# Thresholded attention, then a squared-ReLU layer on one core: one chain of weight sums moved across the end of each pass, and sums of x moved by one or two products

## The chip, the cores and the metric

The kernel runs on one core of a Trainium2 chip. The metric is the device time of one execution in microseconds (us), lower is better. Before the change three runs took 1284.32 to 1285.13 us, with a median of 1284.76. The engines are PE (TensorE, matmuls and their weight loads), DVE (VectorE), ACT (ScalarE), POOL (GpSimd) and SP (SyncE, which here only issues DMAs). Each engine executes its own instructions in the order in which the program lists them; semaphores make one wait for another.

## The reference

```python
scores = scale * np.matmul(q, k.transpose(0, 1, 3, 2))        # 8 x 8 heads of 576 x 64
thresh = np.max(scores, axis=-1, keepdims=True) - tau
scores = np.where(scores >= thresh, scores, -1000000000.0)
attn = softmax(scores)                                        # with 1e-9 added to the sum
x = matmul(attn, v), heads joined to 4608 tokens x 512
h = np.maximum(x @ w_in, 0.0)                                 # 512 -> 2048
out = (h * h) @ w_out                                         # 2048 -> 512
```

Everything is float32.

## The kernel before, in words

The kernel has three stages: attention (to about 494 us of the profile), the first layer (x times w_in, 494 to 884 us), and the second layer (to the end). The change lies in the first layer.

Both layers multiply in Winograd's form of Strassen's scheme, in two levels: a 2 x 2 block product is made of 7 products instead of 8, at the price of sums of blocks ahead of it and behind it. With two levels there are 7 x 7 = 49 products, an outer index m and an inner index k. The loop over m goes in the order `OUTER = (1, 2, 6, 7, 4, 5, 3)`, and within one m the function `inner` (line 734) takes k in the order 1, 6, 7, 5, 2, 4, 3.

The 4608 tokens are taken in nine passes of 49 products; product 7i + j of a pass is the j-th of the i-th m. A product of passes 1 to 6 is 4 matmul instructions of 256 columns on the profile, one of passes 0, 7 and 8 is 8 of 128 columns. Passes 1 and 2 share one set of x (set 1), passes 3 and 4 set 2, passes 5 and 6 set 3; pass 7 has set 4.

Within one m the four PSUM banks X, Y, Z and W are used as follows. Product 0 fills X, and ACT copies it out (`p1`, line 769). Product 1 fills Y, and DVE adds p1 to it (`u2`). Product 2 fills Z, and DVE adds u2 (`u3`). Product 3 fills W, and DVE adds u3. Product 4 adds into X, product 5 into Z, product 6 into W, each followed by a DVE addition. So product 5 of an m, which writes into Z again, must wait until DVE has read Z for u3; product 6 must wait until DVE has read W. These DVE additions are line 128 with `ph` as input. Results that also need a kept sum get a POOL addition (line 128 on POOL, 128 x 512). m = 1 has none of these, m = 5 has six, the others three. The m of 2, 4, 5 and 3 give outputs: each output is put through ReLU and Square by ACT (lines 916 and 917) five products later and stored by SP (line 920).

Three kinds of extra work ride along, at product numbers written out by hand:

- *Chains of weight sums* (`chain_out`, line 1179). For the second layer's weights 44 chains run during the first layer: SP loads four 128 x 128 blocks at the chain's first product (line 1191), POOL makes four subtractions at its products 6, 7, 8 and 9 (line 1194, which shows as line 125, 128 x 128), and SP stores four blocks at its product 10 (line 1196). Two buffers alternate, so a chain's load waits until the store of the chain two before it has landed. `CHAINS` (line 1177) begins chains at products 0, 6, 12, 18, 24 and 30 of a pass (in pass 0 only the last three, in pass 7 the first five).
- *Sums of x* (`plan` and `summed`, lines 1200 to 1214). Set i + 1 is summed while set i is in use, from product 8 of a pass with an even number on, and on through the first products of the set's own first pass ("54" is product 5 of the next pass). Each sum has two steps: ACT copies one operand into PSUM (`c`, line 879) at the product written in the plan, and DVE subtracts (line 125 with `c`) two products later, or at the next sum's number if that comes sooner. There are two `c` buffers. In a plan's entry, `out_` is a sum of outer blocks, `in_` a sum of inner blocks of the m's named, and the last numbers name the sum.
- *Loads of x* (`load_set`, line 824, shown as line 837) on SP's queue. For sets 2 and 3 they stand at products 35 of the pass before, 7, 21 and 28.

Within one product's tick the order in the program is: chain instructions, DVE steps of sums that are due, new loads of x and new ACT copies, and then at most one ReLU and Square with its store.

Of the kernel before, what the change touches and what calls it, by code (L numbers as in the profile page):

```python
# [48 lines left out]
def kernel(  # L49
# [38 lines left out]
    NSTEP = B * S // STEP  # L88
# [75 lines left out]
    def made_at(m):  # L164
        return 4 + MADE.index(m) if m in MADE else RAW.index(m)
# [961 lines left out]
    with tc.manual_schedule():  # L1127
# [46 lines left out]
        chain_at = 26 * BANK  # L1174
        chains = [((0, RAW.index(k)), c) for k in RAW for c in range(4)]
        chains += [((1, made_at(m)), c) for c in range(4) for m in OUTER]
        CHAINS = [49 * n + 6 * c for n in range(NSTEP - 1) for c in range(3 if n == 0 else 0, 6)][0 : len(chains)]
        QUARTER = BANK // 4
        def chain_out(n, tick):

            for c, begins in enumerate(CHAINS):
                s_ = 49 * n + tick - begins
# [17 lines left out]
        def plan(i, at, loads, work):  # L1200
            for t, ms in loads.items():
                NEXT.setdefault(at + t, []).append(lambda ms=ms: load_set(i, ms))
            for t, (what, *args) in work.items():
                NEXT.setdefault(at + t, []).append(lambda what=what, args=args: summed(lambda: what(i, sum_v, *args)))
# [7 lines left out]
        def summed(copied):  # L1212
# [1 line left out]
            open_sum.append((clock["n"], copied()))  # L1214

        out_, in_ = sum_outer, sum_inner
        tail = {
            54: (out_, 4, 0), 56: (in_, (6, 7), 5), 58: (in_, (6, 7), 6), 60: (in_, (6, 7), 7), 62: (in_, (6, 7), 4), 65: (out_, 4, 1),
            68: (in_, (4, 5), 5), 70: (in_, (4, 5), 6), 72: (in_, (4, 5), 7), 74: (in_, (4, 5), 4),
            78: (in_, (3,), 5), 81: (in_, (3,), 6), 83: (in_, (3,), 7), 85: (in_, (3,), 4),  # L1220
        }
        plan(1, 0, {0: (7, 1, 3, 2)}, {
            10: (in_, (1,), 5), 12: (in_, (1,), 6), 14: (in_, (1,), 4), 16: (out_, 5, 0), 19: (out_, 5, 1), 21: (in_, (1,), 7),
            23: (out_, 6, 0), 26: (out_, 6, 1), 29: (out_, 7, 0), 31: (out_, 7, 1),
# [2 lines left out]
        for i in (2, 3):  # L1227
            plan(i, (2 * i - 2) * 49, {-14: (1,), 7: (7,), 21: (2,), 28: (3,)}, {
                8: (in_, (1,), 5), 10: (in_, (1,), 6), 12: (in_, (1,), 4), 15: (out_, 5, 0), 18: (out_, 5, 1), 21: (in_, (1,), 7),
                27: (in_, (2,), 5), 29: (in_, (2,), 6), 31: (in_, (2,), 7), 33: (in_, (2,), 4),  # L1230
                35: (out_, 6, 0), 37: (out_, 7, 0), 39: (out_, 6, 1), 41: (out_, 7, 1), **tail,
            })
        four = (1, 7, 2, 3)
        plan(4, 6 * 49, {-14: (1, 7), 7: (3, 2)}, {
# [124 lines left out]
```

## Time and profile before

| | |
|---|---|
| median of three runs | 1284.76 us |
| the profiled execution | 1284.26 us |
| span from its first to its last instruction | 1282.3 us |
| PE busy in the span | 1254.7 us, 98% |
| DVE, ACT, POOL busy | 999.9, 856.0, 895.6 us |
| first layer, from 493.99 to 884.23 us | 390.24 us, PE busy 388.23 |
| in it DVE, ACT, POOL busy | 305.60, 254.54, 325.86 us |

A row of the timeline gives the start, the length, the engine, the line, the operation with what it writes and reads, how many like it follow without a break (x3), and in brackets the idle time of the engine ahead of it with what ended that idle time. A row of the windows gives a stretch and its length, the busy time of an engine in it with the number of instructions, the granted TensorE clock, the mean busy share of the DMA engines and what they moved.

### The profile page before, as it was taken

The numbers are of one execution on the slowest core, as the hardware profiler recorded it, in microseconds if no ns is written. First come the engines' busy times: TensorE is split into PE (matmuls) and PEld (weight loads), VectorE is DVE, ScalarE is ACT, GpSimd is POOL, SyncE is SP. The second block draws the span as 40 slices with busy tenths as digits, with TensorE's granted clock in tenths as the row PEclk, the third lists the DMA queues.
The fourth block names the chain that finished last, engine by engine and source line by source line (L and its number), as shares of the span: only waits on it lengthen the run. The fifth ranks groups of instructions, "written<-read, shape, count | busy, mean of one in ns | idle before, by whom it ended". The sixth has DMA issues, their size and how long they took to land. (4 is left out here: it accounts for less than half of the span.)

```text
span 1282.3 us, 44206 instructions
## 1 busy us (share of the span) xinstructions
PE 1254.7 (98%) x17459; PEld 1086.2 (85%) x17459; DVE 999.9 (78%) x2449; ACT 856.0 (67%) x1552; POOL 895.6 (70%) x1094
## 2 busy tenths in 40 slices
PE   8998999999999999999999999999999999999998
PEld 6666666677777768988888788999999999999998
DVE  6999999999999997787878777877745664565463
ACT  6999999999999995666765766667423431343240
POOL 2565655655555557888797889758777867786775
PEclk9999999999999999999999999999999999999999
DMA  5565666544333413556666566589645314522411
GB/s 151 156 157 158 159 197 185 147 96 113 89 82 83 99 33 98 166 166 213 190 194 207 174 197 190 173 311 396 214 132 165 125 54 153 165 87 84 161 35 33
DMA packets 256591, 191.89 MB, mean 150 GB/s; under 512 B 96000, under 2 KB 217344, under 8 KB 256384
## 3 DMA queue, kind: packets, MB, share of 16 engines
q1 hardware_dynamic: 254928, 188.63, 49.3%
q8 instruction: 137, 2.24, 0.7%
q14 instruction: 70, 0.57, 0.1%
q10 hardware_dynamic: 1456, 0.44, 0.1%
HBM read 116.65 MB, written 72.35 MB: 147 GB/s over the span
## 5 line engine op out<-in xcount | busy, mean ns | idle before, releaser
L128 POOL TENSOR_TENSOR arena<-arena 128x512 f32<-128x512 f32 (+1 forms) x314 | 377.6, 1221 | 129.6 <-DVE arena L128 100.2
L1085 PE MATMUL po<-wall,arena 128*128 128x128 f32 x3528 | 394.4, 275 | 0.2 <-DVE arena L125 0.2
L1085 PEld LDWEIGHTS po<-wall,arena 128*128 128x128 f32 x3528 | 394.1, 192 | 0.4 <-DVE arena L125 0.4
L946 PE MATMUL ph<-arena,wall 128*128 128x128 f32 (+1 forms) x2352 | 388.2, 328 | 2.5 <-DVE arena L128 1.4
L946 PEld LDWEIGHTS ph<-arena,wall 128*128 128x128 f32 x2352 | 354.1, 191 | 36.6 <-DVE arena L128 4.5
L128 DVE TENSOR_TENSOR arena<-ph,arena 128x512 f32<-128x512 f32 x378 | 255.2, 689 | 76.4 <-PE ph L946 47.3
L125 POOL TENSOR_TENSOR arena<-arena 128x128 f32<-128x128 f32 (+2 forms) x314 | 254.8, 812 | 29.6 <-DMA arena<-w 11.2
L879 ACT COPY c<-arena 128x512 f32<-128x512 f32 (+2 forms) x319 | 176.1, 558 | 105.3 <-DVE arena L125 87.6
L128 DVE TENSOR_TENSOR arena<-po,arena 128x128 f32<-128x128 f32 x378 | 108.4, 290 | 168.3 <-PE po L1085 168.0
L473 ACT ACTIVATE arena<-arena 128x576 f32<-128x576 f32 x288 | 225.7, 871 | 17.4 <-DVE arena L463 17.4
L478 DVE SCALAR_TENSOR_TENSOR arena<-arena 128x576 f32<-128x576 f32 x288 | 225.8, 813 | 0.8 <-POOL arena L470 0.8
L463 DVE TENSOR_SCALAR_CACHE_REDUCE arena<-sc 128x576 f32<-128x576 f32 x288 | 204.4, 752 | 14.0 <-ACT arena L535 6.5
L125 DVE TENSOR_TENSOR arena<-arena,c 128x512 f32<-128x512 f32 (+2 forms) x283 | 177.0, 634 | 9.8 <-ACT c L879 8.7
L544 PEld LDWEIGHTS sc<-arena 64*64 64x64 f32 x5760 | 144.4, 133 | 44.7 <-DVE arena L463 42.1
L445 PE MATMUL sc<-arena 64*64 64x64 f32 (+1 forms) x2304 | 169.3, 415 | 1.8 <-DVE arena L665 1.7
L544 PE MATMUL sc<-arena 64*64 64x128 f32 (+1 forms) x5760 | 160.5, 262 | 10.3 <-DVE arena L463 7.8
L535 ACT COPY arena<-pt 128x1024 f32<-128x1024 f32 x144 | 159.2, 1105 | 1.6 <-PE pt L388 1.5
L769 ACT COPY arena<-po 128x128 f32<-128x128 f32 x63 | 16.6, 263 | 185.4 <-PE po L1085 185.4
L388 PEld LDWEIGHTS pt<-ident,arena 64*128 64x128 f32 x2304 | 83.0, 139 | 41.7 <-ACT arena L535 33.5
L445 PEld LDWEIGHTS sc<-arena 64*64 64x64 f32 x2304 | 62.1, 133 | 48.8 <-issue 22.8
L388 PE MATMUL pt<-ident,arena 64*128 64x64 f32 x2304 | 100.8, 227 | 2.4 <-ACT arena L535 2.0
L470 POOL TENSOR_SCALAR arena<-arena,tau_p 128x2 f32<-128x2 f32 x144 | 65.2, 453 | 41.9 <-DVE arena L463 35.1
(51 smaller groups left out, 919.4 us busy)
## 6 DMA issues: line engine op xcount, KB each, us to landing
g<-arena SPq DMA_DIRECT2D x144, 256.0 KB, 2.6
arena<-g SPq DMA_DIRECT2D x144, 256.0 KB, 5.0
w<-arena SPq DMA_DIRECT2D x60, 256.0 KB, 2.6
wall<-w SPq DMA_DIRECT2D x49, 256.0 KB, 5.3
arena<-w SPq DMA_DIRECT2D x44, 256.0 KB, 3.0
arena<-in_v_dram SPq DMA_DIRECT2D x32, 288.0 KB, 3.8
out_dram<-arena SPq DMA_DIRECT2D x70, 128.0 KB, 2.5
arena<-in_q_dram SPq DMA_DIRECT2D x64, 128.0 KB, 3.8
```

Source lines behind the costliest of these rows:

```text
L125: e.tensor_tensor(out=out, in0=x, in1=y, op=ALU.subtract)
L128: e.tensor_tensor(out=out, in0=x, in1=y, op=ALU.add)
L388: made = nc.tensor.transpose(pt[:, r, ts(slot, HALF)], of[rows, :], ident[rows, rows])
L445: made = nc.tensor.matmul(sc[at, ds(to, count)], lhs, kT[rows, ds(at_k, count)], start=True, stop=True)
L463: made = nc.vector.tensor_scalar(out=s[:, j, :], in0=sc[:, ds(at, S)], scalar1=1.0, scalar2=None, op0=ALU.mult, op1=ALU.min, accum_out=nmx ...
L473: nc.scalar.activation(out=w[:, :, j, :], in_=of(j), func=AF.Exp, bias=nmx[:, j : j + 1], scale=-1.0)
L478: nc.vector.scalar_tensor_tensor(out=w[:, :, j, :], in0=of(j), scalar=thr[:, j : j + 1], in1=w[:, :, j, :], op0=ALU.is_le, op1=ALU.mult, a ...
L535: touch("weights", nc.scalar.copy(joined(to), whole(pt, 0, count)), at, 2 * BANK, m)
L544: made = nc.tensor.matmul(sc[ds(u * D, D), ds(5 * j * BANK + row, count)], loaded_v[i][rows, (c - (u != j)) % CH, :], wT[m][rows, ds(weigh ...
L879: nc.scalar.copy(c, y)
L946: nc.tensor.matmul(to[:, j, :], W_IN[m, k][:, ts(h * parts_ + j, P)], x_of(m, k), start=(not more and j == 0), stop=True, skip_group_check ...
L1085: nc.tensor.matmul(to, g[:, j, :], w[:, j, :], start=(not more and j == 0), stop=(j == 3), skip_group_check=True)
```

## The change

The sixth chain of each pass begins at product 43 instead of product 30. Its load is then issued at product 43, its four subtractions fall on products 0 to 3 of the next pass, and its store on product 4 there. The number of chains, their order and their buffers stay.

The sums of x that change their product are, in the numbers of the plan: in the tail of all three sets 54 to 53 (first half of outer sum 4), 65 to 67 (its second half), 74 to 73 (inner sum 4 of m = 4 and 5) and 81 to 79 (inner sum 6 of m = 3); for sets 2 and 3 also 27 to 26 (inner sum 5 of m = 2), 37 to 38 and 41 to 40 (the two halves of outer sum 7). The plan of set 4 stays.

```diff
-        CHAINS = [49 * n + 6 * c for n in range(NSTEP - 1) for c in range(3 if n == 0 else 0, 6)][0 : len(chains)]
+        BEGINS = (0, 6, 12, 18, 24, 43)
+        CHAINS = [49 * n + BEGINS[c] for n in range(NSTEP - 1) for c in range(3 if n == 0 else 0, 6)][0 : len(chains)]
...
-        tail = {
-            54: (out_, 4, 0), 56: (in_, (6, 7), 5), 58: (in_, (6, 7), 6), 60: (in_, (6, 7), 7), 62: (in_, (6, 7), 4), 65: (out_, 4, 1),
-            68: (in_, (4, 5), 5), 70: (in_, (4, 5), 6), 72: (in_, (4, 5), 7), 74: (in_, (4, 5), 4),
-            78: (in_, (3,), 5), 81: (in_, (3,), 6), 83: (in_, (3,), 7), 85: (in_, (3,), 4),
-        }
+        tail = {53: (out_, 4, 0), 56: (in_, (6, 7), 5), 58: (in_, (6, 7), 6), 60: (in_, (6, 7), 7), 62: (in_, (6, 7), 4), 67: (out_, 4, 1), 68: (in_, (4, 5), 5), 70: (in_, (4, 5), 6), 72: (in_, (4, 5), 7), 73: (in_, (4, 5), 4), 78: (in_, (3,), 5), 79: (in_, (3,), 6), 83: (in_, (3,), 7), 85: (in_, (3,), 4)}
...
         for i in (2, 3):
             plan(i, (2 * i - 2) * 49, {-14: (1,), 7: (7,), 21: (2,), 28: (3,)}, {
                 8: (in_, (1,), 5), 10: (in_, (1,), 6), 12: (in_, (1,), 4), 15: (out_, 5, 0), 18: (out_, 5, 1), 21: (in_, (1,), 7),
-                27: (in_, (2,), 5), 29: (in_, (2,), 6), 31: (in_, (2,), 7), 33: (in_, (2,), 4),
-                35: (out_, 6, 0), 37: (out_, 7, 0), 39: (out_, 6, 1), 41: (out_, 7, 1), **tail,
+                26: (in_, (2,), 5), 29: (in_, (2,), 6), 31: (in_, (2,), 7), 33: (in_, (2,), 4), 35: (out_, 6, 0), 38: (out_, 7, 0), 39: (out_, 6, 1), 40: (out_, 7, 1), **tail,
             })
```

## The prediction

> **What bounds the kernel now.** I read the page first, then the stretch of each pass in the windows, and then the timeline of the engines just ahead of the places where PE stands.
>
> ```profile
> span 1282.3 us, 44206 instructions
> ```
>
> The profiled execution took 1284.26 us, so 1.96 us lie around its span; it is 0.50 us below the median of 1284.76.
>
> ```profile
> 493.99:538.13 44.14, 44.11 (x393) 1.00 0.46 143
> 538.13:580.62 42.49, 42.49 (x198) 1.00 0.61 190
> 580.62:623.65 43.03, 42.58 (x198) 1.00 0.67 204
> 623.65:666.86 43.21, 42.92 (x197) 1.00 0.60 185
> 666.86:709.89 43.03, 42.57 (x197) 1.00 0.68 207
> 709.89:753.84 43.95, 43.16 (x197) 1.00 0.60 184
> 753.84:796.35 42.51, 42.51 (x198) 1.00 0.60 182
> 796.35:884.23 87.88, 87.88 (x785) 1.00 0.79 274
> 580.62:620.34 39.72, 39.72 (x186) 1.00 0.66 201
> 840.30:883.17 42.87, 42.87 (x386) 1.00 0.99 363
> ```
>
> These are windows of PE's first-layer matmuls: passes 0 to 6 one by one, passes 7 and 8 together, then two stretches in which nothing disturbs PE. The undisturbed ones give the pace: 46 products of pass 2 in 39.72 us, 0.8635 each, and 48 products of pass 8 in 42.87, 0.893 each. So 49 products need 42.31 us in passes 1 to 6 and 43.76 in the others. Against that the passes lose 0.38, 0.18, 0.72, 0.90, 0.72, 1.64 and 0.20 us (0 to 6), and 7 and 8 together 0.36. The granted clock is 1.00 everywhere. PE is the bound, and all that rescheduling the layer's side work can bring is 5.1 us. The question is which engine is late at the few places where those 5.1 us arise, and whether the moved steps are in its queue.
>
> In an even pass the place is product 47 (m = 3, its product 5), which waits for u3. First the rows of DVE, then of ACT, then of PE in pass 2 and in pass 4:
>
> ```profile
> 618.42 0.68 DVE L125 TENSOR_TENSOR arena<-arena,c 128x512 f32<-128x512 f32 x1
> 619.88 0.69 DVE L128 TENSOR_TENSOR arena<-ph,arena 128x512 f32<-128x512 f32 x1 [0.78 <-ACT arena L769]
> 620.49 0.68 DVE L125 TENSOR_TENSOR arena<-arena,c 128x512 f32<-128x512 f32 x1
> 621.08 2.11 DVE L128 TENSOR_TENSOR arena<-ph,arena 128x512 f32<-128x512 f32 x3
> 618.75 0.58 ACT L879 COPY c<-arena 128x512 f32<-128x512 f32 x1
> 619.27 0.58 ACT L769 COPY arena<-ph 128x512 f32<-128x512 f32 x1
> 621.82 1.13 PE L946 MATMUL ph<-arena,wall 128*128 128x256 f32 x4 [0.46 <-DVE arena L128]
> 708.06 1.13 PE L946 MATMUL ph<-arena,wall 128*128 128x256 f32 x4 [0.46 <-DVE arena L128]
> ```
>
> At the pace above product 47 of pass 2 would start at 580.62 + 47 x 0.8635 = 621.20; it starts at 621.82, 0.62 late, and 0.72 - 0.62 = 0.10 more is lost on the matmuls behind the wait. DVE stood idle for 0.78 us until p1 (619.27) had come, did u2 (619.88), then a sum of x (620.49, the second half of outer sum 7, "41" of the plan), and only then u3 (621.08). ACT copies that sum's operand at 618.75, before p1.
>
> In passes 3 and 5 the place is products 12 to 16, and the cause lies before the pass's end, on POOL. Around the start of pass 5 (709.89), POOL's rows:
>
> ```profile
> 702.38 1.00 POOL L125 TENSOR_TENSOR arena<-arena 128x128 f32<-128x128 f32 x2
> 703.33 2.52 POOL L128 TENSOR_TENSOR arena<-arena 128x512 f32<-128x512 f32 x2
> 705.79 1.01 POOL L125 TENSOR_TENSOR arena<-arena 128x128 f32<-128x128 f32 x2
> 706.76 8.66 POOL L128 TENSOR_TENSOR arena<-arena 128x512 f32<-128x512 f32 x7
> ```
>
> The four short ones (702.38, 705.79) are the sixth chain's subtractions, in a queue that runs without a gap from there to 715.42. The seven long ones are additions of m = 5 and 3, whose outputs ACT squares. ACT in pass 5, then in pass 3:
>
> ```profile
> 710.53 0.63 ACT L916 ACTIVATE arena<-arena 128x512 f32<-128x512 f32 x1 [0.90 <-POOL arena L128]
> ...
> 712.99 0.63 ACT L916 ACTIVATE arena<-arena 128x512 f32<-128x512 f32 x1 [0.69 <-POOL arena L128]
> ...
> 718.74 0.58 ACT L769 COPY arena<-ph 128x512 f32<-128x512 f32 x1
> ```
> ```profile
> 623.55 0.63 ACT L916 ACTIVATE arena<-arena 128x512 f32<-128x512 f32 x1 [0.16 <-POOL arena L128]
> ...
> 626.02 0.63 ACT L916 ACTIVATE arena<-arena 128x512 f32<-128x512 f32 x1 [0.70 <-POOL arena L128]
> ```
>
> ACT waits twice for POOL (0.90 + 0.69, 0.16 + 0.70), has no idle time after that, and so reaches p1 of product 7 late (718.74). From there DVE works without a break to the inner sum that product 16 reads:
>
> ```profile
> 719.44 1.51 DVE L128 TENSOR_TENSOR arena<-ph,arena 128x512 f32<-128x512 f32 x2
> 724.45 0.68 DVE L125 TENSOR_TENSOR arena<-arena,c 128x512 f32<-128x512 f32 x1
> 725.28 0.89 PE L946 MATMUL ph<-arena,wall 128*128 128x256 f32 x3 [0.22 <-DVE arena L125]
> 638.30 0.89 PE L946 MATMUL ph<-arena,wall 128*128 128x256 f32 x3 [0.22 <-DVE arena L125]
> ```
>
> Product 16 starts at 725.28 against 709.89 + 16 x 0.8635 = 723.71, 1.57 late; in pass 3 at 638.30 against 637.47, 0.83 late. Some 0.07 follows in both.
>
> **The change part by part.**
>
> *Outer sum 7, second half: copy from 41 to 40, with 37 to 38 ahead of it (passes 2 and 4).* The copies are the same four before p1, and ACT's squares in that stretch too, so p1 stays at 619.27. But the DVE step now comes after product 42 instead of 43, ahead of u2. It can start when its copy ends, 618.75 + 0.58 = 619.33, in the 0.78 us in which DVE stood idle. The sum before it (618.42) changes places with one addition; both take the same time. DVE's steps start 0.60 apart, so u2 starts at about 619.97 (p1 is ready at 619.85) and u3 at 620.57, 0.51 before 621.08. Product 47 then starts at 621.31, still 0.11 late. Gain 0.51 in pass 2. Pass 4 shows the same wait of 0.46, and I take the same: together 1.02 us.
>
> *The sixth chain's subtractions.* From 702.38 to 703.33 and from 705.79 to 706.76 they hold up POOL by 0.95 + 0.97 = 1.92 us. Without them the seven additions end 1.92 earlier, which covers both waits of ACT. A wait costs ACT some 0.08 more than its idle time, since a follower otherwise starts before the one ahead has ended (619.27 follows 618.75 by 0.52, and that lasts 0.58). So p1 of product 7 comes 0.90 + 0.69 + 0.16 = 1.75 us earlier in pass 5 and 0.16 + 0.70 + 0.16 = 1.02 in pass 3. The subtractions reappear at products 0 to 3, where m = 1 gives POOL no additions: from about 713.50 to 715.42, the time at which POOL ends its row now. That costs nothing as long as the four of the pass's first chain, which follow, wait for their load anyway.
>
> *54 to 53.* Today this sum's DVE step stands just ahead of u2 (719.44), which p1 (718.74 + 0.58 = 719.32) would let start 0.10 sooner. One product earlier it is out of the way: 0.10 in passes 1, 3 and 5.
>
> *Passes 3 and 5 together.* Each starts 0.51 earlier. Product 16 of pass 5 can start at 725.28 - 1.75 - 0.10 = 723.43, PE arrives at 723.71 - 0.51 = 723.20: 0.23 late, with 0.07 behind it 0.30 instead of 1.64, a gain of 1.34. Pass 3: 638.30 - 1.12 = 637.18 against 636.96, 0.22 + 0.07 = 0.29 instead of 0.90, a gain of 0.61. Pass 1 gains 0.10 of its 0.18.
>
> *The chain's DMAs on SP.* The load moves from 30 to 43, where the buffer's last store (product 28) has long landed, so it does not wait; a wait at 30 is gone. The store moves to product 4 of the next pass, in front of one output's store; and the load at product 6 must now wait until it has landed, with everything behind it on SP. Rows of this (SP's waits from 538 to 797 us, the load's issue in pass 2, and the listing of the DMAs of those passes):
>
> ```profile
> SPq L1191 <- DMA w<-arena: 48.9, 24, 4.6
> 588.70 0.60 SPq L1191 DMA_DIRECT2D arena<-w  x1
> w<-arena SPq DMA_DIRECT2D x36, 256.0 KB, 2.4
> ```
>
> SP reaches that load only at 588.70, 8.08 us after the pass's start. The subtractions will end about 715.42 - 709.89 = 5.5 us after a pass's start, and a store issued then lands by its median of 2.4 us at 7.9, in time; after the longest wait of 4.6 us at 10.1, 2 us late. I take nothing, by the median, and keep up to 2 us of lateness for the rivals.
>
> The Trainium skill's page DMA: Bandwidth & Descriptors, in its section on the anatomy of one DMA, puts a DMA at about 2.0 us fixed plus its bytes at 436 GB/s; for 256 KB that is an estimate of 2.6 us, and by it the load would never be late and the sum would stand with no loss at all. The measured longest wait of 4.6 us contradicts that as a bound, and the measurement decides: the loss stays among the rivals.
>
> *27 to 26, 65 to 67, 74 to 73, 81 to 79.* Nothing. The first only makes ACT wait one product longer for x (row below). The others are finished at most one product later or sooner, and their readers come at least one product after that; what covers them is DVE's and ACT's idle time in the second half of odd passes, where PE has no wait. If that cover were gone, each would cost one DVE step, 0.6 us.
>
> *Passes 0, 6, 7 and 8.* Their 0.94 us stay: pass 0's and 6's are the same wait at product 47, but their plans keep 41.
>
> The sum: 1.02 + 0.61 + 1.34 + 0.10 = 3.07 us. From 1284.26 that is 1281.2; at the median 1284.76 - 3.07 = 1281.7 us.
>
> **The rivals.**
>
> *ACT is its own limit.* POOL's relief does not reach p1, because squares that come earlier find ACT busy with others. Then passes 3 and 5 keep their loss and gain 0.10 each; 1.02 + 0.30 = 1.3, so 1283.4. For it: ACT has no idle time between 712.99 and 718.74. Against it: the idle times of 0.90 and 0.69 name POOL.
>
> *The even passes' slot brings nothing*, because the operand's copy comes later than now and u2 waits behind its sum. Then passes 3 and 5 start at their old time; product 16 is ready before PE arrives (723.43 against 723.71), their whole 1.64 + 0.90 goes, with 0.10 in pass 1: 1282.1.
>
> *Slower: x comes late.* The new wait at product 6 holds SP, and the loads of x at products 7 and 21 stand behind it. ACT already waits for the one of product 21, and p1 of product 28 right behind it:
>
> ```profile
> 605.71 0.38 ACT L879 COPY c<-arena 128x256 f32<-128x256 f32 x1 [4.77 <-DMA arena<-xT]
> 607.72 1.51 DVE L128 TENSOR_TENSOR arena<-ph,arena 128x512 f32<-128x512 f32 x2
> ```
>
> u3 of product 30 (607.72) is read at about 608.4; product 33 starts at 580.62 + 33 x 0.8635 = 609.12, so 0.7 us are spare. Each us of lateness beyond 0.7 is a us of PE in passes 2 and 4. A wait of the mean 48.9 / 24 = 2.0 passed on whole costs 2 x 1.3 = 2.6, the longest of 4.6 costs 7.8; between them 5.2, which gives 1284.76 - 3.07 + 5.2 = 1286.9. It decides from 0.7 + 3.07 / 2 = 2.2 us of lateness on. Against it: SP is late at that load anyhow, and the chain's next stores wait for POOL, which absorbs some.
>
> **How the numbers follow.** The forecast, 1280.6 to 1282.8, has 0.57; ACT's own limit 0.17; the slot without effect 0.12; late x 0.12; 0.02 is left for a second half of the gain that I miss (all but passes 0, 6, 7 and 8 clean: 4.2 us, 1280.6). About 0.2% (2.6 us) is what a measurement of this kernel tells from no change, so faster means below 1282.2. The forecast lies 0.5 us inside that bound, the slot case on it. Faster 0.57 (0.50 of the forecast, 0.05 of the slot case, the 0.02), slower 0.06 (half of late x, whose upper half passes 1287.3), the same 0.37. The range: 1280.2 to 1285.2, which takes in the rivals up to half of the late-x case.
>
> **What would show it.** The windows of passes 2 and 4 at 42.5, of pass 3 at 42.6 and of pass 5 at 42.6; no wait of ACT's line 916 for POOL at the starts of passes 3 and 5; four short POOL instructions after the seven long ones; the DVE sum at the end of passes 2 and 4 in front of u2. It is wrong if ACT's wait for x ahead of product 28 grows by over 0.7 us, if new waits of PE stand near product 33, or if the first chain's load in a pass is issued over 2 us later than now.

## The result, and the profile after

The changed kernel took 1281.35 us, the median of 22 runs (1279.94 to 1285.35), against 1283.72 us in 22 runs of the kernel before (1281.95 to 1287.09). The ratio is 0.9979, with a 95% interval from 0.9973 to 0.9985: 2.7 us less, between 1.9 and 3.5 (the two medians lie 2.4 apart). The profiled execution took 1280.43 us, 3.83 less than the one of before.

First the windows of PE's first-layer matmuls in the changed kernel: passes 0 to 6 one by one, then 7 and 8 together. The columns are those of the prediction's windows.

```profile
492.59:536.73 44.14, 44.11 (x392) 1.00 0.44 137
536.73:579.21 42.48, 42.48 (x198) 1.00 0.61 188
579.21:622.31 43.10, 42.84 (x197) 1.00 0.69 204
622.31:664.95 42.64, 42.54 (x197) 1.00 0.62 189
664.95:707.66 42.71, 42.57 (x197) 1.00 0.67 207
707.66:750.14 42.48, 42.48 (x197) 1.00 0.63 192
750.14:792.64 42.50, 42.50 (x197) 1.00 0.59 182
792.64:880.53 87.89, 87.89 (x785) 1.00 0.80 280
```

The first layer takes 880.53 - 492.59 = 387.94 us instead of 390.24: 2.30 us less, of the predicted 3.07. Pass 5 gives 1.47, pass 3 0.57, pass 4 0.32 and pass 1 0.01; pass 2 loses 0.07. What lies behind the layer is as long as before (398.07 us, before 398.08). The remaining 1.4 us of the two spans' difference lie ahead of it: the first layer began at 493.99 us before and begins at 492.59 now. The change does not touch that stage. In the twelve executions of the experiments its end lies between 492.7 and 496.0 without order, which alone spreads single times by over 3 us. So below I compare the length of the first layer, pass by pass, and not single times.

What was predicted for the sixth chain is there. POOL's rows around the start of pass 5 (707.66), then ACT's row of p1 of product 7:

```profile
701.21 9.92 POOL L128 TENSOR_TENSOR arena<-arena 128x512 f32<-128x512 f32 x8
711.10 4.08 POOL L125 TENSOR_TENSOR arena<-arena 128x128 f32<-128x128 f32 x8
```
```profile
715.03 0.57 ACT L769 COPY arena<-ph 128x512 f32<-128x512 f32 x1
```

POOL's additions run without a subtraction between them, and the eight short steps behind them are the moved chain's four and the next chain's four. ACT's squares no longer name POOL. p1 comes 715.03 - 707.66 = 7.37 us after the pass's start; before it was 718.74 - 709.89 = 8.85.

What was predicted for passes 2 and 4 came only in part. DVE near the end of pass 2, then ACT ahead of product 28 in that pass:

```profile
618.35 0.69 DVE L125 TENSOR_TENSOR arena<-arena,c 128x512 f32<-128x512 f32 x1 [0.26 <-ACT c L879]
618.95 2.90 DVE L128 TENSOR_TENSOR arena<-ph,arena 128x512 f32<-128x512 f32 x4
```
```profile
605.53 0.38 ACT L879 COPY c<-arena 128x256 f32<-128x256 f32 x1 [5.99 <-DMA arena<-xT]
```

The sum (618.35) now stands ahead of u2 (618.95), in the time in which DVE stood idle. Yet product 47 still loses 0.30 + 0.10 us in both passes (0.62 + 0.10 before). And in pass 2 the wait for x has grown from 4.77 to 5.99 us; product 33 came 0.29 late there, and 0.10 followed. That ate pass 2's gain. (The 0.10 is lost on the matmuls just behind a wait.)

### The profile page after: what moved, and what is told of

It reads as the page before. It is cut to its first block, busy times and chain, and to the rows that moved or that the text cites. A ratio compares the mean times of both kernels' runs of the same rounds, so it can differ in the third digit from the quotient of the medians.

```text
span 1278.6 us, 44201 instructions
## 1 busy us (share of the span) xinstructions
PE 1255.2 (98%) x17459; PEld 1087.0 (85%) x17459; DVE 1000.2 (78%) x2449; ACT 855.6 (67%) x1552; POOL 897.4 (70%) x1094
## 4 chain that ended last, share of the span: by engine, by line
PE 70%; DMA 1%; ACT 1%; DVE 1%; issue 1%; ACTq 0%; DVEq 0%; SPq 0%
PE po L1085 30%; PE ph L946 27%; PE sc L544 5%; PE sc L445 4%; PE pt L388 2%; DMA wall<-w 1%; PE sc L406 1%; PE sc L388 1%; DVE arena L128 1%; DVE arena L463 0%; DMA g<-arena 0%; ACT arena L916 0%; ACT c L879 0%; DMA arena<-xT 0%; ACT arena L917 0%
## 5 line engine op out<-in xcount | busy, mean ns | idle before, releaser
L473 ACT ACTIVATE arena<-arena 128x576 f32<-128x576 f32 x288 | 232.1, 918 | 16.7 <-DVE arena L463 16.7
L535 ACT COPY arena<-pt 128x1024 f32<-128x1024 f32 x144 | 166.0, 1153 | 1.6 <-PE pt L388 1.5
```

Of the source, the lines that this page charges most:

```text
L473: nc.scalar.activation(out=w[:, :, j, :], in_=of(j), func=AF.Exp, bias=nmx[:, j : j + 1], scale=-1.0)
L535: touch("weights", nc.scalar.copy(joined(to), whole(pt, 0, count)), at, 2 * BANK, m)
```

## The experiments

**Both kernels once more**, unedited, for what varies by itself:

> The kernel before once more, to see how far the losses of its passes repeat. If they come from the order of the work, the lengths of passes 1 to 6 repeat within 0.1 us (42.49, 43.03, 43.21, 43.03, 43.95, 42.51), and what differs between executions lies in the attention stage. If they come from chance in the DMAs, passes 2 to 5 differ by several tenths.

> The changed kernel once more. By the theory that the order of the work sets the losses, passes 1 to 6 repeat their lengths (42.48, 43.10, 42.64, 42.71, 42.48, 42.50) within 0.1 us. The new wait of 0.4 us at product 33 of pass 2 hangs on when a load of x lands; if that is chance, pass 2 comes out at 42.7 instead of 43.1.

Passes 2 and 3 of the kernel before, then of the changed one:

```profile
581.72:624.95 43.23, 42.77 (x197) 1.00 0.67 203
624.95:668.80 43.85, 43.08 (x198) 1.00 0.59 181
```
```profile
580.96:624.96 44.00, 43.11 (x198) 1.00 0.68 201
624.96:667.86 42.90, 42.68 (x198) 1.00 0.61 188
```

The layer took 390.19 us before and 389.11 after. Passes 0, 1 and 4 to 8 repeat to 0.02 us, but for pass 5 of before (43.07 here, 43.95 first). Passes 2 and 3 do not: the kernel before took 43.21 us in pass 3 at first and 43.85 here. In pass 2 the changed kernel lost 0.9 us more than in its first profile. The kernel before lost 0.20 us at product 33 here, so a late x there is no new thing. The changed kernel's extra loss stands at products 46 and 47, and POOL's rows show from where:

```profile
612.86 0.46 POOL L125 TENSOR_TENSOR arena<-arena 128x128 f32<-128x128 f32 x1 [3.78 <-DMA arena<-w]
```

The load of the chain that begins at product 24 came late: it waited on SP for the store of the chain two before it (issued at 603.21, load issued at 607.81) and then took 5 us itself. POOL stood for 3.78 us with its additions behind that subtraction, the squares came late, and p1 of product 42 with them.

The same wait of POOL, shorter, stands in the kernel before as well, and it goes with the length of the odd pass that follows. Here it is ahead of passes 3 and 5, in the first profile and in the second:

```profile
609.76 0.45 POOL L125 TENSOR_TENSOR arena<-arena 128x128 f32<-128x128 f32 x1 [1.01 <-DMA arena<-w]
696.91 0.46 POOL L125 TENSOR_TENSOR arena<-arena 128x128 f32<-128x128 f32 x1 [1.92 <-DMA arena<-w]
```
```profile
611.86 0.46 POOL L125 TENSOR_TENSOR arena<-arena 128x128 f32<-128x128 f32 x1 [2.03 <-DMA arena<-w]
697.92 0.46 POOL L125 TENSOR_TENSOR arena<-arena 128x128 f32<-128x128 f32 x1 [1.00 <-DMA arena<-w]
```

Behind waits of 1.01 and 1.00 us the odd pass took 43.21 and 43.07, behind 1.92 and 2.03 it took 43.95 and 43.85. So what an odd pass loses in the kernel before seems to depend on when a load of weights lands, and it changes from one execution to the next. These are four passes, and no run moves that load alone.

**One half of the change at a time.** Each half ran twice, on two chips.

```diff
 chain alone: the tail and the plan of sets 2 and 3 as before
-        tail = {53: (out_, 4, 0), ...
+        tail = {54: (out_, 4, 0), ...
-   26: (in_, (2,), 5), ... 38: (out_, 7, 0), 39: (out_, 6, 1), 40: (out_, 7, 1), **tail,
+   27: (in_, (2,), 5), ... 37: (out_, 7, 0), 39: (out_, 6, 1), 41: (out_, 7, 1), **tail,
 sums alone: the chains as before
-        BEGINS = (0, 6, 12, 18, 24, 43)
-        CHAINS = [49 * n + BEGINS[c] for n in ...
+        CHAINS = [49 * n + 6 * c for n in ...
```

> Only the sixth chain moves, the sums of x stay. My theory: passes 3 and 5 fall from 43.21 and 43.95 to about 42.6 and 42.5 to 42.7, passes 2 and 4 keep their 0.7 us at product 47, and pass 2 shows the new wait at product 33 (0.4), so 43.1 to 43.5. The rival that ACT is its own limit: passes 3 and 5 stay at 43.1 to 43.9. The rival that the new wait at product 33 comes from the sums (27 to 26): none there.

> The chain's move alone, once more. If the chain is what frees passes 3 and 5, they come out at 42.48 again, and the layer at 388.0 to 388.3; if that was chance in the DMAs, one of them is above 43.

> Only the sums of x move, the chain stays. My theory: passes 2 and 4 fall from 43.03 to 42.7 (the wait at product 47 from 0.6 to 0.3), passes 3 and 5 keep at least 43.0 and 43.7, no wait at product 33. The rival that the chain at products 36 to 39 also holds the work ahead of product 47: passes 2 and 4 stay near 43.0. The rival that the sums alone bring the gain: passes 3 and 5 fall to 42.6 as well.

> The moved sums alone, once more. By my theory pass 4 repeats 42.71, passes 3 and 5 lie at 43 or above, and the layer at 389.5 to 391; the 0.84 us at product 4 of pass 3 of the first look came with a late landing in pass 2 and need not repeat. By the rival that the sums' new places cause it, it repeats.

Passes 2 to 5 with the chain alone; then pass 2 of its second run; then passes 2 to 5 with the sums alone, first run:

```profile
581.65:624.68 43.03, 42.58 (x198) 1.00 0.69 206
624.68:667.15 42.47, 42.47 (x197) 1.00 0.62 190
667.15:710.18 43.03, 42.57 (x197) 1.00 0.67 204
710.18:752.66 42.48, 42.48 (x198) 1.00 0.61 186
```
```profile
580.77:624.80 44.03, 43.10 (x198) 1.00 0.66 200
```
```profile
579.91:623.04 43.13, 42.66 (x197) 1.00 0.65 198
623.04:667.87 44.83, 43.42 (x197) 1.00 0.59 183
667.87:710.59 42.72, 42.58 (x198) 1.00 0.68 207
710.59:753.75 43.16, 42.87 (x198) 1.00 0.61 189
```

With the chain alone the layer took 388.03 and 389.18 us, with the sums alone 390.85 and 390.34. The chain carries the gain: passes 3 and 5 fall to 42.5 (42.62 in pass 3 of the second run), and passes 2 and 4 keep the 43.03 of before. The second run has the same late load in pass 2 as the changed kernel's second profile (POOL idle for 3.51 us). The sums alone shorten pass 4 by 0.31 and bring the layer nothing: passes 3 and 5 together take 88.0 and 87.8 us, against 87.2 and 86.9 in the two profiles of before, and ACT's squares at their starts still wait for POOL. In the first of the two runs ACT also waited 1.18 us in pass 3 for a store of outputs to land. So what an even pass gains the next odd one gives back while the chain stands in POOL's row. On top of the chain's move the sums brought only 0.1 us in each of two profiles (387.94 and 389.11 for the whole change): the 0.32 that pass 4 gains is mostly lost again in passes 2 and 3.

**Is it POOL's time, or the place of the chain's DMAs?** The kernel before, with the sixth chain's loads and stores where they were, and only its four subtractions left out (so the weight sums of those chains are not made).

```diff
-                if 6 <= s_ < 10:
+                if 6 <= s_ < 10 and begins % 49 != 30:
```

> The kernel before, with the sixth chain's four subtractions left out and its load and store kept (so those weight sums are not computed). It takes away 1.9 us of POOL's queue ahead of the seven additions and nothing else. My theory (POOL's queue makes ACT late): passes 3 and 5 fall to 42.5 to 42.7, passes 2 and 4 keep 0.7 us at product 47, no wait at product 33. The rival that it is the chain's place in SP's queue, not POOL's time, that counts: passes 3 and 5 stay at 43.2 and 43.9.

Passes 3 and 5, and POOL around the start of pass 5 (708.47):

```profile
622.97:665.45 42.48, 42.48 (x198) 1.00 0.61 190
...
708.47:750.95 42.48, 42.48 (x197) 1.00 0.61 187
```
```profile
700.47 11.14 POOL L128 TENSOR_TENSOR arena<-arena 128x512 f32<-128x512 f32 x9 [0.30 <-ACT arena L916]
713.24 2.06 POOL L125 TENSOR_TENSOR arena<-arena 128x128 f32<-128x128 f32 x4 [1.62 <-DMA arena<-w]
```

The layer took 388.03 us, as in the first run with the chain alone, and each pass agrees with it to 0.01 us. So the gain is that of four POOL steps (1.9 us in each pass) taken out of a row that ACT waits for; between these two profiles the moved DMAs make no difference. In their new place the subtractions cost nothing.

**A third buffer for the chains**, taken from the ring of output buffers (the eight that the outputs use in turn), so that a chain's load waits for the store of the chain three before it.

```diff
-    hid.ring("o", [BANK * i for i in range(18, 26)])
+    hid.ring("o", [BANK * i for i in range(18, 25)])
-                t = arena[:, ds(chain_at + (c % 2) * BANK, BANK)]...
+                t = arena[:, ds(chain_at + (c % 3 - 1) * BANK, BANK)]...
```

> The changed kernel with three buffers for the chains instead of two (one is taken from the eight output buffers), so that a load no longer waits for a store issued two products earlier. My theory for the new wait at product 33 of pass 2: loads of x stand on SP behind the load at product 6, so it goes, and pass 2 falls from 43.10 to 42.7. The rival that x lands late because the DMA engines are full: it stays at 43.1. By both, passes 3 to 6 stay.

Passes 2 and 4, then PE's waits behind the first layer:

```profile
580.03:622.75 42.72, 42.58 (x198) 1.00 0.69 206
...
665.22:707.93 42.71, 42.57 (x198) 1.00 0.68 204
```
```profile
PE po L1085 <- POOL arena L125: 2.4, 1, 2.4
```

Pass 2 is as short as pass 4 now, and the layer takes 387.62 us. The load of x for product 28 is issued 20.17 us after the pass's start, where the changed kernel's came at 21.08 in its first profile: the chain's loads ahead of it no longer wait. The same holds in every later run with three buffers, none of which has a late pass 2. But a late issue is not all of it: in the changed kernel's second profile the load was issued at 20.33, and ACT still got its x only at 26.22 (26.32 in the first). Against the gain, 0.2 us are lost in pass 8, and 2.4 us where the second layer begins. Both are gone in the last version below, which has eight buffers in the ring again from pass 8 on. That points to the shorter ring; by which path it delays POOL's sum I did not trace.

**The sum behind u3 instead of ahead of u2**: in the changed kernel, the second half of outer sum 7 at 43 instead of 40. That leaves u2 and u3 side by side, and it also takes the sum's copy on ACT from ahead of p1 to behind it.

```diff
-   ... 39: (out_, 6, 1), 40: (out_, 7, 1), **tail,
+   ... 39: (out_, 6, 1), 43: (out_, 7, 1), **tail,
```

> The changed kernel with the second half of outer sum 7 at 43 instead of 40, so that ACT copies its operand behind p1 of product 42 and DVE does it behind u3. My theory for the 0.4 us left at product 47 of passes 2 and 4: u3 starts 0.79 behind u2, which it reads, and p1 stands behind the sum's copy (0.52). With the copy gone p1, u2 and u3 come about 0.5 earlier, the wait of 0.3 goes, and pass 4 falls from 42.71 to 42.31 to 42.4, pass 2 from 43.10 to 42.7. The rival that p1 is held by the squares ahead of it, so that the copy's place does not matter: both stay.

Passes 2 to 5, then PE and ACT in pass 3:

```profile
582.62:624.93 42.31, 42.31 (x198) 1.00 0.68 206
624.93:667.76 42.83, 42.61 (x197) 1.00 0.62 190
667.76:710.06 42.30, 42.30 (x197) 1.00 0.68 208
710.06:752.89 42.83, 42.61 (x197) 1.00 0.62 191
```
```profile
639.20 3.04 PE L946 MATMUL ph<-arena,wall 128*128 128x256 f32 x13 [0.22 <-DVE arena L125]
```
```profile
630.98 0.59 ACT L879 COPY c<-arena 128x512 f32<-128x512 f32 x1
...
632.70 0.57 ACT L769 COPY arena<-ph 128x512 f32<-128x512 f32 x1
```

Passes 2 and 4 run at the undisturbed pace, with no loss at all. In pass 4, p1 of product 42 comes 38.13 us after the pass's start (38.64 in the changed kernel), since the copy no longer stands ahead of it; u3 still follows u2 by 0.79. Of the 0.41 us that pass 4 gains against the changed kernel, pass 5 gives 0.35 back, at product 16. The pass starts sooner, ACT has no idle time any more, and it reaches p1 of product 7 only 7.77 us after the pass's start (7.37 to 7.58 in the changed kernel). Here ACT is its own limit, and one of the steps ahead of p1 is the copy at 630.98, that of the sum at 53. The layer takes 387.27 us.

**Everything together.** With three buffers, the slot at 43 in all plans, and the first half of outer sum 4 out of ACT's way:

```diff
-        tail = {53: (out_, 4, 0), 56: (in_, (6, 7), 5), 58: (in_, (6, 7), 6), 60: (in_, (6, 7), 7), 62: (in_, (6, 7), 4), 67: (out_, 4, 1), ...
+        tail = {53: (in_, (6, 7), 5), 56: (in_, (6, 7), 6), 58: (in_, (6, 7), 7), 61: (in_, (6, 7), 4), 64: (out_, 4, 0), 66: (out_, 4, 1), ...
```

> The changed kernel with three buffers, the sums of 40 or 41 at 43 in all plans, and the inner sums of m = 6 and 7 ahead of outer sum 4 (53, 56, 58, 61, then 64 and 66). My theory: the waits at products 47 of passes 0, 2, 4 and 6 (0.3, 0.4, 0.4, 0.2), at 33 of pass 2 (0.4) and at 16 of passes 1, 3 and 5 (0.2, 0.35, 0.2) go, so the first layer falls by 2.0 to 2.4 us against the changed kernel's 387.94, and the time to about 0.9964 of the kernel before. The rival that removing one wait only brings out the next, as at product 33: the layer falls by less than 1 us.

In this order the inner sums of m = 6 and 7 ran ahead of outer sum 4 and overwrote blocks that it reads, so part of the sums of x has other values; the number and size of all instructions stay. The layer took 386.34 us (even passes 42.31, odd ones 42.52 to 42.58), the kernel 1280.11 us, a ratio of 0.9963 (0.9950 to 0.9977). The next version keeps outer sum 4 ahead of those that overwrite its blocks, behind p1 of product 7, and gives pass 8 the eight output buffers back, since the chains have ended by then:

```diff
+        tail = {56: (in_, (6, 7), 5), 57: (out_, 4, 0), 58: (in_, (6, 7), 6), 59: (in_, (6, 7), 7), 61: (in_, (6, 7), 4), 67: (out_, 4, 1), ...
...
+            if last:
+                hid.ring("o", [BANK * i for i in range(18, 26)])
```

> As the run with all moves, but with the sums of m = 6, 7 and 4 in an order that keeps every operand (56, 57 for the first half of outer sum 4, 58, 59, 61, then 67), and with eight output buffers again in pass 8, whose lack I hold for the cause of the new wait at the start of the second layer. My theory: no wait at products 47, 33 and 16, the first layer at 385.6 to 386.4 us, the rest at 398.1, the time at 0.9955 to 0.9965 of the kernel before. The rival that seven output buffers are not the cause: the rest stays at 399 to 400.

The windows of passes 7 and 8, then POOL and PE early in pass 8:

```profile
791.19:835.14 43.95, 43.95 (x393) 1.00 0.61 192
835.14:885.16 50.02, 45.73 (x394) 0.97 0.95 332
```
```profile
853.66 1.26 POOL L128 TENSOR_TENSOR arena<-arena 128x512 f32<-128x512 f32 x1 [15.11 <-DMA g<-arena]
```
```profile
854.78 5.48 PE L946 MATMUL ph<-arena,wall 128*128 128x128 f32 x33 [4.29 <-DVE arena L128]
```

Passes 0 to 6 were as hoped, pass 8 took 6.1 us more, and the whole came out slower than the kernel before: 1285.68 us, a ratio of 1.0016 (1.0007 to 1.0025). POOL waited for stores of outputs (g<-arena). The last four outputs of pass 7 lay in the ring of seven at places whose banks are 23, 24, 18 and 19, and their stores stand on SP behind sixteen loads (issued from 846.5 to 848.5 us, and landed over 5 us later). Pass 8 began its new ring at 18, with two of those. One edit tests that:

```diff
-                hid.ring("o", [BANK * i for i in range(18, 26)])
+                hid.ring("o", [BANK * i for i in (25, 20, 21, 22, 23, 24, 18, 19)])
```

> The previous kernel (e7_all_mended) with one edit: in pass 8 the ring of output buffers begins with the four that the last outputs of pass 7 do not hold (banks 25, 20, 21, 22, and only then 23, 24, 18, 19). Theory: the 6.1 us of pass 8 came from the first outputs of pass 8 sharing buffers with the last four of pass 7, whose stores are issued behind sixteen loads on SP. Then pass 8 returns to 43.95 us, passes 1 to 6 stay at 42.3 to 42.4, the first layer takes 385.8 us against 390.2 of the kernel before, the rest of the span behind it 398.1, and the time is about 4.4 us less than before, a ratio of 0.9966. Rival: the wait stands on the loads themselves, or on POOL, and not on the ring's order: then pass 8 stays near 50 us and the time near the kernel before's.

Its windows (passes 1, 2 and 8):

```profile
536.55:578.94 42.39, 42.39 (x198) 1.00 0.64 191
578.94:621.25 42.31, 42.31 (x198) 1.00 0.69 206
...
834.59:878.52 43.93, 43.93 (x394) 1.00 0.99 363
```

Pass 8 is back, and the layer takes 385.82 us, 4.42 less than before the change and 2.12 less than after it. The kernel took 1278.40 us (five runs, 1278.02 to 1279.51) against 1283.84 on the same chip: a ratio of 0.9960 (0.9946 to 0.9974), or 5.1 us less than before (3.3 to 6.9). Of the ceiling of 5.1 us that the windows of before gave for the layer, some 0.7 are left.

## Why the prediction was right, and where its terms were off

The direction, the mechanism and the time held: 3.07 us less were forecast, 2.7 (1.9 to 3.5) were measured. By its own steps:

*What bounds the kernel.* Right. What was gained in the layer was gained at the places named, and the last experiment reached most of the ceiling.

*The sixth chain's subtractions.* Right in cause: leaving the subtractions out gave the same passes as moving the chain, so the cause is shown, not only argued. That they cost nothing at products 0 to 3 held as well. The size was met in part by luck. In the profiles from which it was worked out, pass 5 gained 1.47 (1.34 predicted) and pass 3 0.57 (0.61). In the second profiles of both kernels they gained 0.59 and 0.95: 1.54 together, where 1.95 was predicted and 2.04 came first. The prediction took the losses of one execution as fixed, and they are not.

*Outer sum 7, "gain 0.51" in each even pass.* Right in mechanism, too large in size: 0.32 in pass 4, and 0.32 at product 47 of pass 2. The step that failed is "DVE's steps start 0.60 apart". u3 reads what u2 has written, and in the changed kernel it starts 0.79 behind it (618.95, 619.74, inside the row of four). Before, the sum stood between the two and used that time. The prediction had quoted the sign of it: u2 and u3 in one row, 1.51 long, while two other additions take 1.28 (rows below). The same difference, 0.19, is what the forecast had too much. The forecast also left the sum's copy on ACT ahead of p1. With the sum behind u3 the distance of 0.79 stays, and the loss goes because p1 and u2 come earlier; so that run shows the better place, and the rows show the distance.

*54 to 53, "0.10 in passes 1, 3 and 5".* It brought nothing: pass 1 went from 42.49 to 42.48. p1 of product 7 in that pass, in the changed kernel, then DVE's rows behind it:

```profile
544.12 0.57 ACT L769 COPY arena<-ph 128x512 f32<-128x512 f32 x1
```
```profile
544.80 1.51 DVE L128 TENSOR_TENSOR arena<-ph,arena 128x512 f32<-128x512 f32 x2 [0.54 <-ACT arena L769]
546.24 0.68 DVE L125 TENSOR_TENSOR arena<-arena,c 128x512 f32<-128x512 f32 x1
546.83 1.28 DVE L128 TENSOR_TENSOR arena<-ph,arena 128x512 f32<-128x512 f32 x2
...
549.82 0.68 DVE L125 TENSOR_TENSOR arena<-arena,c 128x512 f32<-128x512 f32 x1
```

The sum is out of the way, and yet u2 starts 544.80 - 536.73 = 8.07 us after the pass's start, where it was 546.22 - 538.13 = 8.09 before. The step that failed is that p1 "would let [u2] start 0.10 sooner": p1 ends at 544.12 + 0.57 = 544.69, and u2 follows 0.11 later with nothing between them. So that 0.1 was the way from ACT to DVE and not the sum's. From u2 on DVE works to the sum that product 16 reads (549.82), and a floor of 0.17 us stays in passes 1, 3 and 5. In the last two kernels, which put the first half of outer sum 4 at 57, they take 42.39.

*The chain's DMAs on SP, "nothing, up to 2 us late".* In both profiles of the changed kernel the load at product 6 was issued 8.67 us after the pass's start (587.88 - 579.21 in the first), where it was 8.08 and 8.35 before, since the store ahead of it landed after 2.8 us. SP's waits for such stores are the same in sum:

```profile
SPq L1192 <- DMA w<-arena: 47.9, 24, 4.7
```

Before it was 48.9, 24 and 4.6. In the Trainium skill's page DMA: Bandwidth & Descriptors, the section on the anatomy of one DMA gives its 2.0 us and bytes at 436 GB/s as a fit for DMAs that GpSimd issues. The DMAs here are issued by SP, so the estimate of 2.6 us for them was carried over from another path; the longest wait of 4.7 us here again speaks against taking it as a bound.

*The rival "x comes late".* In part, and two of the three signs by which the prediction would be wrong did appear in pass 2: ACT's wait for x grew by 1.22 us (4.77 to 5.99), where 0.7 was the limit, and PE waited at product 33. The third did not, since the first chain's load was issued 0.6 us later than in the first profile of before and not 2. The price was 0.29 + 0.10 us in the profiled execution and 0.19 + 0.10 in the second one, and not the 1.3 or more that the rival needed. The runs do not tie it to the moved chain. In the first profile the load of x stood behind a load of weights that waited 3.3 us for the earlier store from its buffer to land (2.5 before), and both belong to chains that did not move. With two buffers product 33 loses something in two of the five profiles with the sixth chain in its old place and in three of the five with it moved, and with three buffers in none of four.

A different lateness behind the same two buffers, that of the load at product 24, brought pass 2 to 44.00 us once in the changed kernel and to 44.03 once with the chain alone, against 43.10 and 43.03 in their first profiles. POOL's wait for that load was 3.78 and 3.51 us in these two, and 1.0 to 2.9 in the other eight profiles with two buffers. Whether the moved chain makes the long waits more likely these few cannot settle; with three buffers POOL did not wait there.

*The rivals "ACT is its own limit" and "the slot brings nothing".* Neither came. The first came true one step later, when the even passes lost nothing any more. One reading of the plans was wrong but changes nothing: of passes 0 and 6, which the prediction left out because they "keep 41", pass 0 follows a plan that has 40 there.

The sum in the layer: 0.57 + 1.47 + 0.32 + 0.01 and the 0.07 lost in pass 2 make 2.30 where 3.07 stood: 0.38 of the difference is u3's distance to u2, 0.39 the late x of pass 2, 0.09 what 54 to 53 did not bring in pass 1, and 0.09 came on top in passes 3 and 5. In the second pair of profiles the layer gained only 1.08 (390.19 to 389.11), with the late load in pass 2. The 2.7 of the 22 runs (1.9 to 3.5) lies nearer the first pair; how often the late load came among those runs is not known.

## What to carry to other kernels

An engine that is far from busy (POOL, 70% of the span) can still set the pace through a queue: look at which of its instructions stand ahead of the one that somebody waits for, and move those that nobody waits for behind it. Before a step is put into an idle gap, ask what stood in the gap it leaves: here it had filled a delay between two dependent steps, and the better place was behind both. A loss read from one execution is not a fixed amount: profile the same kernel twice before its pieces are added up. And when a ring of buffers changes its length, go through the slots that the last users still hold before the next stage begins with them.

## What the runs showed of the hardware

- On DVE two additions of 128 x 512 start 0.60 us apart when independent, and 0.79 (u2 at 618.95, u3 at 619.74) when the second reads what the first has written. The Trainium skill's page VectorE: DVE Perf Modes, in the section The DRAIN you can't avoid, reports that eight copies took equally long with a semaphore after each and with one after the last, so that the semaphore cost nothing extra there. The 0.19 us between these two distances do not fit a reading by which a dependent follower is free; which part of them is a semaphore's, no run here separates.
- A wait costs PE more than its idle time in the rows: 0.30 us at product 47 with 0.14 idle, 0.62 with 0.46 before. In the rows a matmul of 256 columns lasts 0.38 us and the next one starts 0.22 after it; the 0.16 between are the difference. The matmul behind the wait then lasts 0.48, and the one after it starts 0.32 behind it instead of 0.22: that is the 0.10 that follows these waits, at a granted clock of 1.00.
- Stores and loads of the same 256 KB took from 2.3 to 5.1 us to land in passes 2 and 4, and with two alternating buffers pass 2 of one and the same kernel took 43.10 and 44.00 us, or 43.03 and 44.03.
